# Token-ordered rows with indirect loads, column sums of the first weights off TensorE, and a sixth key/value slot in a fused attention and Fourier feed-forward kernel

## The chip, the cores and the metric

The kernel runs on one core of one Trainium2 chip. The metric is the device time of one launch in microseconds (us). A core has TensorE (PE in the profile; PEld is its weight load), VectorE (DVE), ScalarE (ACT), GpSimd (POOL) and SyncE (SP), which issues most DMAs. Each engine works through its own queue in order.

## The reference

Two stages follow one another. The first is linear attention with a norm over each head, the second mixes each sequence by a two-dimensional Fourier transform, normalises each row, and adds a feed-forward of width 2048. All is float32; 8 sequences of 576 tokens, 8 heads of 64, model width 512. The weights come as float64.

```python
kv = np.einsum('bhsd,bhse->bhde', k, v)
out = np.einsum('bhsd,bhde->bhse', q, kv)
rms = np.sqrt(np.mean(out * out, axis=-1, keepdims=True) + 1e-06)
out = out / rms * g_norm                      # -> x, (8, 576, 512)
...
X = np.fft.fft(np.fft.fft(x, axis=1), axis=2)
u = x + np.real(X)
mu, var = u.mean(-1), u.var(-1)
un = (u - mu) / np.sqrt(var + 1e-06)
ch = np.maximum(un @ w_ch1, 0.0) @ w_ch2
return u + ch
```

## The kernel before, in words

**Two phases.** Phase one takes the sequences one after the other: key/value products (`plan_kv`), query turns (`plan_q`), attention output (`plan_out`), head norm (`plan_y`, `plan_fold`), the transform along the sequence (`plan_seq`) and along the channels (`plan_chn`). The finished rows u go to a DRAM scratch `u_scr`, and their transposes (`plan_turn`) as a high and a low float32r part into blocks of 512 tokens, `unTh` and `unTl`; nine blocks in all. A feed-forward product is three matmuls, high by high, high by low, low by high (`passes`, `ffn1` L341, `ffn2` L360). While phase one runs, `plan_early` already multiplies each finished block by the first three of sixteen feed-forward slices (`NA = 3`) and saves the partial sums. Phase two is the loop at L1168: over segments (block, first slice, last slice); each step makes one slice of the hidden layer (`first`, 12 matmuls of 512 columns) and multiplies the slice of the step before by the second weights (`second`, 12 more).

**The halves of a sequence.** Phase one keeps a sequence as two halves, s = 1..288 in rising order and s = 575..289 in falling order, so that the transform can use the symmetry of sine and cosine (`side` 0 and 1). Before the change that order stays: `u_scr`, the token blocks, the partial sums and the mean row `p0c` all have the second half of each sequence reversed, and the true place is restored at the very end. `ascending(t)` (L224) tells whether a tile of 128 rows lies wholly in first halves; 12 of the 36 tiles do. Those are stored by a direct DMA from SP (L1157); the other 24 by an indirect DMA from POOL (L1159) which scatters rows by `rowidx`.

**The weights.** Each weight slice arrives as float64 words and is turned to float32 by a copy on ACT and six operations on DVE (`w_clear` L281, `w_steps` L283, a total). From a slice of the first weights the mean over the 512 inputs is taken off, since the row mean then need not be subtracted from u: `w_mean` (L302) multiplies each of the four 128-column pieces by a matrix of 1/512 and sums them in PSUM (four float32 matmuls, which the trace shows as eight records), `w_center` subtracts on DVE. Then ACT copies the high part and DVE (phase one, L850) or POOL (phase two, L1071) makes the low part. In phase one this is `plan_w` (L822), for slices 0 to 2 at the start and 3 to 6 once the queries, keys and values are through; in phase two `load_w`, `sum_w` and `split_w` (L1048 to L1071) for slices 7 to 15, one weight slice a step over the first 18 steps.

**What sets the order.** Phase one is written down as operations with a cost, a rank and the buffers they need, and a planner (`Plan`, L54) simulates the engines at build time: at every moment each engine takes the ready operation of lowest rank for which ring slots are free, and the program is emitted in that order. Ring sizes stand in `RINGS` (L37): five slots `kv` of 256 KB for keys and values, two slots `wk` for work tiles of weights, eight PSUM banks `p8`. Phase two is a plain loop. The framework then schedules the emitted program by a simulation of its own and adds the waits. Phase two's rows are read back from `u_scr` (`load_u` L1099), in a ring `uu` of eight tiles, that is, two blocks; their variance is taken on DVE (L1107), and POOL adds in the scaled early partial sums (L1119). After the last slice of a block DVE adds the product (L1153) and the tile is stored.

Of the kernel before, what the change touches and what calls it, by code (L numbers as in the profile page):

```python
# [9 lines left out]
F32 = mybir.dt.float32  # L10
# [21 lines left out]

PAD_LEFT = 32
# [4 lines left out]
    "p8": 8, "part": 2, "unT": 2, "h": 2 * NA, "qt": 2, "fq": 4, "kvt": 2, "kv": 5, "kr": 2,  # L38
# [15 lines left out]
class Plan:  # L54
# [16 lines left out]
    def op(self, eng, cost, rank, emit, after=(), bufs=(), lag=0, port=False):  # L71
        o = Op()
        o.port = port or eng == "POOL"
        o.eng, o.cost, o.rank, o.emit, o.lag = eng, cost, rank, emit, lag
# [14 lines left out]
    def run(self):  # L89
# [20 lines left out]
        while left:  # L110
# [14 lines left out]
            while again:  # L125
                again = False
                for eng, q in ready.items():
# [40 lines left out]
                    for u in users[o.n]:  # L168
                        need[u.n] -= 1
                        if not need[u.n]:  # L170
# [4 lines left out]
                            heapq.heappush(events, (max(at, t), n, "ready", u))  # L175
# [6 lines left out]
def kernel(  # L182
# [119 lines left out]
    def w_mean(ps, af):  # L302
        for c in range(KC):
            nc.tensor.matmul(  # L304
                ps[:, :P], mean_t, af[:, c * P : (c + 1) * P], start=(c == 0), stop=(c == KC - 1)
            )
# [472 lines left out]
    def plan_turn(b, side, t, x, done):  # L779

        n = TR + 1 if side == t == 0 else TR - 1 if side and t == 2 else TR
        r0 = b * S + (HALF + 1 if side else 1) + t
        cols = [(0, min(n, TR), r0, 3)] + [(TR, n, b * S, 1)] * (n > TR)
        pieces = []
        for lo, hi, at, step in cols:
            while lo < hi:
                j = at // BT
                end = min(hi, lo + -(-((j + 1) * BT - at) // step))
# [16 lines left out]
        for j, lo, hi, at, step in pieces:  # L805
            to = slice(at, at + step * (hi - lo - 1) + 1, step)
# [15 lines left out]
    def plan_w(which, f, pool, r, after=(), r_load=None):  # L822
# [11 lines left out]
        d = op("ACT", 670, r, lambda: w_clear(raw.t, ps.t), [a], [raw, ps, pf])  # L834
# [13 lines left out]
        def lo(src):  # L848
            h, l = w_t[which, f]
            nc.vector.tensor_tensor(l, src.t, h.bitcast(F32), ALU.subtract)  # L850

        src = ps
        if which == 1:
            src, mean = ring("wk", one, [P, DM], "wa"), bank_buf("ps_w")
            e = op("DVE", 700, r, lambda: total(src), [d], [src, ps, pf])
            e = op("PE", 870, r, lambda: w_mean(mean.t, src.t), [e], [src, mean])
# [4 lines left out]
        w_done[which, f] = op("DVE", 700, r, lambda: lo(src), [g], [src], port=(which == 1))  # L861
# [117 lines left out]
    def p0_out():  # L979
# [5 lines left out]
        nc.vector.tensor_copy(p0u.t[:B, : HALF - 1], p0t.t[:B, 1:HALF])  # L985
# [66 lines left out]
    def sum_w(which, f):  # L1052
# [7 lines left out]
        sums[which, f] = af  # L1060

    def split_w(which, f):
        af = sums.pop((which, f))
        if which == 1:
            ps = bank("ps_w")
            w_mean(ps, af)
# [71 lines left out]
    def second(seg, hpair, f):  # L1138
        j, f0, f1 = seg
        for i in tiles_of[j]:  # L1140
# [15 lines left out]
            if ascending(t):  # L1156
                nc.sync.dma_start(out[t * P : (t + 1) * P, :], ut)  # L1157
            else:
# [115 lines left out]
```

## Time and profile before

| | |
|---|---|
| median of 3 runs | 1050.78 us (1050.68 to 1051.03) |
| the profiled execution | 1044.39 us, of which the span from first to last instruction is 1042.5 us |
| mean granted TensorE clock | 0.993 |
| TensorE matmul busy | 1003.8 us, 5962 records |
| DVE, ACT, POOL busy | 472.9, 325.7, 310.9 us |
| DMA moved | 140.72 MB |

The page splits the span into 40 slices of 26 us each; a digit gives the busy share in tenths. Phase one fills about the first 15 slices, the loop the rest. Busy times of DVE instructions overlap a little (0.69 us long, started every 0.60 us), so a sum of them is more than the time they take. Some matmul records are missing from the trace, so a PE share just under 1 in a long dense window is not idle time. In the chain of waits the share of an engine says how much of the span it was the last to be ready.

### The profile page before, as it was taken

To read this page: it belongs to the slowest core of one execution; us is meant where nothing else is said; L and a number is where in the kernel's file an instruction comes from. 1 tells how busy PE (TensorE), PEld (TensorE's weight loads), DVE (VectorE), ACT (ScalarE), POOL (GpSimd) and SP (SyncE) were. 2 spreads that over 40 slices of the span, in tenths; PEclk is the share of its full clock that TensorE was granted. 3 is DMA by queue.
4 is the path that set the end of the run, shared out by engine and by line. 5 is a ranking of instruction groups with operands and counts; after the bars stand their busy time and mean duration, and the time that the engine had idled before them with its cause. 6 is when DMAs were issued, how large, how long until landed. Compare 5 with 4: busy or idle time off the path is not lost.

```text
span 1042.5 us, 15216 instructions
## 1 busy us (share of the span) xinstructions
PE 1003.8 (96%) x5962; PEld 847.3 (81%) x5962; DVE 472.9 (45%) x830; ACT 325.7 (31%) x655; POOL 310.9 (30%) x316
## 2 busy tenths in 40 slices
PE   4799999999999899999999999999999999999996
PEld 4687888889878788888888888888888888888884
DVE  4878466667498758887132313131221311311111
ACT  3566556555543334334212022121121121111110
POOL 0466966774662001113813111130020010110000
PEclk9999999999999999999999999999999999999998
DMA  9969688663345845634552414240230400400101
GB/s 251 256 165 283 164 255 243 199 163 130 129 144 201 303 156 194 234 123 141 174 177 75 162 45 158 90 134 20 102 100 1 162 21 1 162 1 1 41 0 41
DMA packets 109195, 140.72 MB, mean 135 GB/s; under 512 B 51790, under 2 KB 76418, under 8 KB 104516
## 3 DMA queue, kind: packets, MB, share of 16 engines
q1 hardware_dynamic: 105588, 132.28, 41.1%
q0 software_dynamic: 1920, 6.29, 1.5%
q10 hardware_dynamic: 1616, 1.18, 0.4%
q8 instruction: 47, 0.77, 0.3%
q14 instruction: 24, 0.20, 0.1%
HBM read 88.33 MB, written 51.40 MB: 134 GB/s over the span
## 4 chain that ended last, share of the span: by engine, by line
PE 88%; DVE 5%; DMA 3%; POOL 2%; issue 1%; ACT 1%; SPq 0%; POOLq 0%; ACTq 0%; DVEq 0%
PE ps_h L345 37%; PE acc L363 37%; PE ps_f L684 3%; PE ps_f L718 3%; PE ps_o L545 3%; PE ps_k L472 2%; PE ps_q L520 1%; PE ps_w L304 1%; PE ps_t L801 1%; DMA vm<-in_v_dram 1%; DMA qt<-in_q_dram 1%; DVE x L642 1%; DVE wp L298 1%; POOL xe L660 0%; DVE ps_a L288 0%
## 5 line engine op out<-in xcount | busy, mean ns | idle before, releaser
L345 PE MATMUL ps_h<-unTh,w 128*128 128x512 f32 x1152 | 357.1, 391 | 0.0
L363 PE MATMUL acc<-w,hh 128*128 128x512 f32 x1152 | 354.7, 393 | 0.0
L358 DVE SCALAR_TENSOR_TENSOR hl<-ps_h,hh 128x512 fp32r<-128x512 f32 x144 | 99.1, 688 | 370.0 <-ACT hh L355 369.8
L363 PEld LDWEIGHTS acc<-w,hh 128*128 128x128 f32 x1152 | 215.9, 189 | 44.7
L345 PEld LDWEIGHTS ps_h<-unTh,w 128*128 128x128 f32 x1152 | 215.0, 188 | 44.0
L355 ACT ACTIVATE hh<-ps_h 128x512 fp32r<-128x512 f32 x144 | 85.8, 596 | 454.3 <-PE ps_h L345 449.0
L345 PE MATMUL ps_h<-unTl,w 128*128 128x512 f32 x576 | 224.5, 390 | 0.0
L363 PE MATMUL acc<-w,hl 128*128 128x512 f32 x576 | 221.3, 391 | 0.0
L1159 POOL DMA_INDIRECT out_dram<-uu,rowidx x24 | 23.4, 975 | 390.4 <-DVE uu L1153 345.1
L363 PEld LDWEIGHTS acc<-w,hl 128*128 128x128 f32 x576 | 108.6, 189 | 22.8
L345 PEld LDWEIGHTS ps_h<-unTl,w 128*128 128x128 f32 x576 | 108.0, 188 | 22.7
L580 POOL TENSOR_TENSOR x<-x,gb 96x512 f32<-96x512 f32 (+1 forms) x48 | 61.1, 1297 | 43.4 <-ACT x L560 43.4
L1119 POOL TENSOR_TENSOR uu<-uu,up 128x512 f32<-128x512 f32 x36 | 45.6, 1292 | 58.2 <-ACT up L1116 58.2
L1071 POOL TENSOR_TENSOR w<-wap,w 128x512 fp32r<-128x512 f32 x18 | 23.0, 1296 | 132.2 <-ACT w L1070 122.7
L545 PE MATMUL ps_o<-kvt,fq 64*96 64x64 f32 (+1 forms) x768 | 45.8, 269 | 1.4 <-ACT fq L524 0.9
L1107 DVE BATCH_NORM_STATS2 bst<-uu 128x6 f32<-128x512 f32 x36 | 24.7, 691 | 48.4 <-DMA uu<-u_scr 48.4
L545 PEld LDWEIGHTS ps_o<-kvt,fq 64*96 64x96 f32 (+1 forms) x768 | 41.9, 180 | 5.3 <-issue 1.4
L1153 DVE SCALAR_TENSOR_TENSOR uu<-acc,rs_yb,uu 128x512 f32<-128x512 f32 x36 | 25.2, 744 | 42.5 <-PE acc L363 42.5
L660 POOL TENSOR_TENSOR xe<-ab 96x256 f32<-96x256 f32 (+1 forms) x48 | 38.8, 834 | 18.4 <-DVE ab L653 12.1
L569 DVE TENSOR_REDUCE ss<-ps_o 96x8 f32<-96x512 f32 (+1 forms) x48 | 31.7, 682 | 22.1 <-ACT ps_o L565 20.5
L472 PE MATMUL ps_k<-vm,km 128*64 128x64 f32 x512 | 27.6, 252 | 13.0 <-DMA vm<-in_v_dram 13.0
L684 PE MATMUL ps_f<-cs,xh 96*128 96x290 f32 (+1 forms) x192 | 39.2, 300 | 0.0
(98 smaller groups left out, 1012.9 us busy)
## 6 DMA issues: line engine op xcount, KB each, us to landing
raw<-in_moe_w_ch_dram SPq DMA_DIRECT2D x32, 512.0 KB
qt<-in_q_dram SPq DMA_DIRECT2D x16, 576.0 KB
unT_scr<-unTh SPq DMA_DIRECT2D x9, 1024.0 KB
unT_scr<-unTl SPq DMA_DIRECT2D x9, 1024.0 KB
part_scr<-part SPq DMA_DIRECT2D x36, 256.0 KB
uu<-u_scr SPq DMA_DIRECT2D x36, 256.0 KB
unTh<-unT_scr SPq DMA_DIRECT2D x9, 1024.0 KB
unTl<-unT_scr SPq DMA_DIRECT2D x9, 1024.0 KB
```

What stands on the lines that cost most here:

```text
L345: nc.tensor.matmul(ps, w[c][:, kc * P : (kc + 1) * P], unT[a][:, kc, :], start=(idx == 0), stop=(idx == 3 * KC - 1),)
L355: nc.scalar.activation(hh, ps, AF.Relu)
L358: nc.vector.scalar_tensor_tensor(hl, ps, 0.0, hh.bitcast(F32), ALU.max, ALU.subtract)
L363: nc.tensor.matmul(acc, hpair[a][:, i * P : (i + 1) * P], w[c], start=(first and n == 0), stop=(last and n == 2),)
L472: nc.tensor.matmul(ps.t[s * D : (s + 1) * D, pr * D : (pr + 1) * D], km[:, s, j, :] if j < 4 else kr[:, h, :], vm[:, s, j, :] if j < 4 els ...
L545: nc.tensor.matmul(pss[s].t[:n, at : at + D], fqs[side].t[half, m, :n], kvt.t[half, m], start=True, stop=True,)
L569: nc.vector.tensor_reduce(ss.t[0][:n, :, t, s::2], pss[s].t[:n].rearrange("p (u m e) -> p u m e", u=2, e=D), AX.X, ALU.add,)
L580: nc.gpsimd.tensor_tensor(v_, v_, gb[:n].unsqueeze(1).to_broadcast([n, H, D]), ALU.mult)
L660: nc.gpsimd.tensor_tensor(o[:, s], a[:, 0], a[:, 1], ALU.subtract if s else ALU.add)
L684: nc.tensor.matmul(ps.t[:, :NS], xs[t].t[a][:n, part, ch * P : (ch + 1) * P], cs[:n, part, c, t, :], start=(idx == 0), stop=(idx == 8),)
L718: nc.tensor.matmul(ps.t[:n, :ND], pt.t[a][:, part, ch, offs[t] : offs[t] + n], cd[:, part, c, ch, :], start=(idx == 0), stop=(idx == 5),)
L1119: nc.gpsimd.tensor_tensor(us[j][i], us[j][i], part, ALU.add)
```

## The change

- The transposes of the second half are written in falling columns (`plan_turn`), and the mean row is reversed once on DVE, so token blocks, partial sums and outputs have the order of the tokens. `u_scr` keeps the old order. All 36 tiles are stored by direct DMAs from SP; the 24 tiles that aren't ascending are instead gathered from `u_scr` by indirect loads on POOL in `load_u`.
- `w_mean` becomes one matmul on a tile of 128 columns. The sum of the four pieces that feeds it is made before: by one DVE reduction for slices 0 to 2 and 7 to 15, by three POOL additions for slices 3 to 6. For slices 3 to 6 POOL also makes the low part of the first weights in place of DVE.
- In the planner, `w_mean` counts as ready 2000 ns later than its input (`SLACK`), and a slice of the first weights claims both of its work tiles at once, at the copy on ACT.
- The ring `kv` has six slots in place of five.

```diff
+SLACK = 2000
...
-    ... "kvt": 2, "kv": 5, "kr": 2,
+    ... "kvt": 2, "kv": 6, "kr": 2,
...
-    def op(self, eng, cost, rank, emit, after=(), bufs=(), lag=0, port=False):
+    def op(self, eng, cost, rank, emit, after=(), bufs=(), lag=0, port=False, wait=0):
...
-                            heapq.heappush(events, (max(at, t), n, "ready", u))
+                            heapq.heappush(events, (max(at, t) + u.wait, n, "ready", u))
...
-    def w_mean(ps, af):
-        for c in range(KC):
-            nc.tensor.matmul(
-                ps[:, :P], mean_t, af[:, c * P : (c + 1) * P], start=(c == 0), stop=(c == KC - 1)
-            )
+    def w_sum(af, to):
+        nc.vector.tensor_reduce(to, af.rearrange("p (c n) -> p n c", c=KC), AX.X, ALU.add)
+
+    def w_sum_pool(af, to):
+        nc.gpsimd.tensor_tensor(to, af[:, :P], af[:, P : 2 * P], ALU.add)
+        for c in range(2, KC):
+            nc.gpsimd.tensor_tensor(to, to, af[:, c * P : (c + 1) * P], ALU.add)
+
+    def w_mean(ps, total):
+        nc.tensor.matmul(ps[:, :P], mean_t, total, start=True, stop=True)
...
-        r0 = b * S + (HALF + 1 if side else 1) + t
-        cols = [(0, min(n, TR), r0, 3)] + [(TR, n, b * S, 1)] * (n > TR)
+        if side:
+            cols = [(0, n, b * S + S - 1 - t, -3)]
+        else:
+            cols = [(0, min(n, TR), b * S + 1 + t, 3)] + [(TR, n, b * S, 1)] * (n > TR)
...
-        d = op("ACT", 670, r, lambda: w_clear(raw.t, ps.t), [a], [raw, ps, pf])
+        src = ring("wk", one, [P, DM], "wa") if which == 1 else ps
+        d = op("ACT", 670, r, lambda: w_clear(raw.t, ps.t), [a], [raw, ps, pf, src])
+        late_ = f >= NA
...
-            nc.vector.tensor_tensor(l, src.t, h.bitcast(F32), ALU.subtract)
+            eng = nc.gpsimd if late_ and which == 1 else nc.vector
+            eng.tensor_tensor(l, src.t, h.bitcast(F32), ALU.subtract)
...
-            e = op("PE", 870, r, lambda: w_mean(mean.t, src.t), [e], [src, mean])
+            if late_:
+                e = op("POOL", 2000, r, lambda: w_sum_pool(src.t, pf.t[:, :P]), [e], [src, pf])
+            else:
+                e = op("DVE", 600, r, lambda: w_sum(src.t, pf.t[:, :P]), [e], [src, pf])
+            e = op("PE", 220, r, lambda: w_mean(mean.t, pf.t[:, :P]), [e], [pf, mean], wait=SLACK)
...
-        nc.vector.tensor_copy(p0u.t[:B, : HALF - 1], p0t.t[:B, 1:HALF])
+        nc.vector.tensor_copy(p0u.t[:B, : HALF - 1], p0t.t[:B, HALF - 1 : 0 : -1])
...
-        sums[which, f] = af
+        if which == 1:
+            w_sum(af, pf[:, :P])
+        sums[which, f] = af, pf[:, :P]
...
-            nc.sync.dma_start(ut, u_scr[n * P : (n + 1) * P])
+            if ascending(n):
+                nc.sync.dma_start(ut, u_scr[n * P : (n + 1) * P])
+            else:
+                nc.gpsimd.indirect_dma_start(
+                    out=ut,
+                    out_offset=None,
+                    in_=u_scr[:NTOK],
+                    in_offset=bass.IndirectOffsetOnAxis(ap=rowidx[:, n : n + 1], axis=0),
+                )
...
-            if ascending(t):
-                nc.sync.dma_start(out[t * P : (t + 1) * P, :], ut)
-            else:
-                nc.gpsimd.indirect_dma_start(
-                    out=out,
-                    out_offset=bass.IndirectOffsetOnAxis(ap=rowidx[:, t : t + 1], axis=0),
-                    in_=ut,
-                    in_offset=None,
-                )
+            nc.sync.dma_start(out[t * P : (t + 1) * P, :], ut)
```

More of the change, by code (lines that the diff above doesn't have):

```diff
@@ L37 @@
 RINGS = {
-    "p8": 8, "part": 2, "unT": 2, "h": 2 * NA, "qt": 2, "fq": 4, "kvt": 2, "kv": 5, "kr": 2,
+    "p8": 8, "part": 2, "unT": 2, "h": 2 * NA, "qt": 2, "fq": 4, "kvt": 2, "kv": 6, "kr": 2,
     "x": 8, "raw": 2, "e2": 4, "wk": 2, "xhl": 3, "pt": 1, "two": 2,
@@ L69, in __init__ @@
         self.now = 0
-    def op(self, eng, cost, rank, emit, after=(), bufs=(), lag=0, port=False):
+    def op(self, eng, cost, rank, emit, after=(), bufs=(), lag=0, port=False, wait=0):
         o = Op()
         o.port = port or eng == "POOL"
+        o.wait = wait
         o.eng, o.cost, o.rank, o.emit, o.lag = eng, cost, rank, emit, lag
@@ L787, in plan_turn @@
                 j = at // BT
-                end = min(hi, lo + -(-((j + 1) * BT - at) // step))
+                last = (j + 1) * BT - 1 if step > 0 else j * BT
+                end = min(hi, lo + (last - at) // step + 1)
                 pieces.append((j, lo, end, at - j * BT, step))
@@ L805, in plan_turn @@
         for j, lo, hi, at, step in pieces:
-            to = slice(at, at + step * (hi - lo - 1) + 1, step)
+            stop = at + step * (hi - lo - 1) + (1 if step > 0 else -1)
+            to = slice(at, None if stop < 0 else stop, step)
             def high(j=j, lo=lo, hi=hi, to=to):
@@ L849, in lo @@
             h, l = w_t[which, f]
-            nc.vector.tensor_tensor(l, src.t, h.bitcast(F32), ALU.subtract)
-        src = ps
+            eng = nc.gpsimd if late_ and which == 1 else nc.vector
+            eng.tensor_tensor(l, src.t, h.bitcast(F32), ALU.subtract)
         if which == 1:
-            src, mean = ring("wk", one, [P, DM], "wa"), bank_buf("ps_w")
+            mean = bank_buf("ps_w")
             e = op("DVE", 700, r, lambda: total(src), [d], [src, ps, pf])
-            e = op("PE", 870, r, lambda: w_mean(mean.t, src.t), [e], [src, mean])
+            if late_:
[3 more added lines that the diff above has]
+            e = op("PE", 220, r, lambda: w_mean(mean.t, pf.t[:, :P]), [e], [pf, mean], wait=SLACK)
             e = op("DVE", 690, r, lambda: w_center(src.t, mean.t), [e], [src, mean])
@@ L860, in plan_w @@
         g = op("ACT", 640, r, lambda: hi(src), [e], [src])
-        w_done[which, f] = op("DVE", 700, r, lambda: lo(src), [g], [src], port=(which == 1))
+        pool_lo = late_ and which == 1
+        w_done[which, f] = op(
+            "POOL" if pool_lo else "DVE", 1340 if pool_lo else 700, r, lambda: lo(src), [g], [src],
+            port=(which == 1),
+        )
     last_first = []
```

5 lines of the change are left out of this document (3 added, 2 removed).

## The prediction, made before the changed kernel was run

> **What bounds the kernel now.** I read the page's busy times and slices first, then the windows by stage, then the waits of TensorE, then the timeline where it waits.
>
> ```profile
> PE 1003.8 (96%) x5962; PEld 847.3 (81%) x5962; DVE 472.9 (45%) x830; ACT 325.7 (31%) x655; POOL 310.9 (30%) x316
> PE   4799999999999899999999999999999999999996
> DVE  4878466667498758887132313131221311311111
> ```
>
> ```profile
> 0.00:58.00 58.00, 37.23 (x388) 33.29 (x390) 33.85 (x55) 25.03 (x50) 19.07 (x31) 1.00 1.00 241
> 58.00:387.00 329.00, 321.36 (x2700) 279.00 (x2697) 230.77 (x421) 171.38 (x393) 179.92 (x192) 0.99 0.63 195
> 387.00:491.00 104.00, 104.00 (x496) 87.17 (x495) 85.90 (x127) 41.92 (x70) 21.70 (x17) 1.00 0.53 178
> 491.00:1031.60 540.60, 540.60 (x2386) 447.61 (x2385) 119.61 (x225) 87.33 (x144) 88.32 (x75) 1.00 0.24 80
> 1031.60:1042.50 10.90, 0.62 (x3) 0.19 (x1) 2.73 (x4) 0.00 (x0) 1.92 (x2) 0.65 0.24 96
> ```
>
> The second fence gives window, length, busy time of PE, PEld, DVE, ACT and POOL with counts, then granted clock, DMA share and GB/s. There are five stages. Up to 58 us TensorE is fed too slowly (37 of 58 us busy) and the DMA engines are full (share 1.00). From 58 to 387 us it is busy for all but 7.6 us. In the two loop windows it is never idle. In the last 10.9 us it has nothing left, and the clock runs on after the last matmul. So time comes out in three ways: matmuls taken off TensorE after 58 us, gaps of TensorE closed, and a shorter end.
>
> **Part 1: the mean of the first weights, in the loop.** Nine slices (7 to 15) lie here.
>
> ```profile
> 407.06 1.06 PE L304 MATMUL ps_w<-wap,mean_t 128*128 128x128 f32 x8
> 407.87 0.70 PE L345 MATMUL ps_h<-unTh,w 128*128 128x512 f32 x2
> 408.11:419.94 11.83, 11.83 (x58) 9.91 (x57) 10.35 (x16) 6.04 (x10) 2.55 (x2) 1.00 0.93 322
> 499.11:509.99 10.88, 10.88 (x49) 9.01 (x49) 1.38 (x2) 4.47 (x6) 10.88 (x10) 1.00 0.61 182
> ```
>
> Two steps with a mean in them take 11.83 us, two without 10.88, so a mean costs 0.95 us. Its eight records start within 407.87 - 407.06 = 0.81 us, 0.101 each; a float32 matmul is two of them, 0.203 us. Three of four go: 0.61 us each, and the remaining 0.34 (one matmul and the change of operands) stays. 9 x 0.61 = 5.5 us. If the whole 0.95 shrinks in proportion, 9 x 0.71 = 6.4.
>
> What is added is a DVE reduction over four pieces 512 bytes apart. No row shows that stride; the nearest is the reduction of adjacent elements below, 680 ns. DVE was busy 10.35 us in the 11.83 (overlaps counted twice). With 0.68 more it is 11.03, against a new TensorE period of 11.83 - 0.61 = 11.22. It fits, narrowly. If the strided read takes twice as long, 1.36, DVE needs 11.71 and becomes the bound: 0.49 x 9 = 4.4 us of the 5.5 are lost. I take 5.5, because 512 elements per partition are read in both; ends 1.1 and 6.4.
>
> **Part 2: the same in phase one.** Slices 2 to 6 lie after 58 us, where other matmuls always wait: 5 x 0.61 = 3.0 us (ends 0, if some other wait eats it, and 3.5). One of the five has a gap in front:
>
> ```profile
> 348.88 2.05 PE L304 MATMUL ps_w<-wa,mean_t 128*128 128x128 f32 x8 [3.42 <-DVE wa L842]
> 345.40:348.90 3.50, 0.08 (x2) 0.05 (x1) 3.40 (x6) 0.60 (x1) 0.00 (x0) 0.99 1.04 438
> 348.90:352.60 3.70, 3.70 (x14) 3.33 (x15) 2.69 (x5) 0.69 (x2) 0.00 (x0) 0.55 0.97 345
> ```
>
> The mean stood at the head of TensorE's queue 3.42 us before DVE had the total, and behind it stood matmuls that could have run. The clock granted afterwards is 0.55 for 3.70 us: another 3.70 x 0.45 = 1.7 us. Together 5.1. The planner's SLACK puts the mean 2.0 us later in the order, so a DVE that is as late as before leaves a gap of 1.4; other matmuls that now come first may close that too. Ends: 5.1 gained, or 5.1 lost, since a new order may leave such a gap elsewhere. I take 3.4, between 2.0 and 5.1. [...]
>
> POOL's share for slices 3 to 6 hides behind its own idleness: it is idle from 345.40 to 352.60 (0.00 twice). Prices:
>
> ```profile
> L569 DVE TENSOR_REDUCE ss<-ps_o 96x8 f32<-96x512 f32 x32 | 21.0, 680 | 14.5 <-ACT ps_o L565 13.0 <-PE ps_q L520 1.5
> L660 POOL TENSOR_TENSOR xe<-ab 96x256 f32<-96x256 f32 x32 | 26.4, 845 | 2.0 <-DVE ab L653 1.3 <-ACT xh L666 0.7
> L609 POOL TENSOR_TENSOR rs_s<-rs_y,m x8: 286/288/291, 42.9 to 285.2; 97x48 f32<-97x48 f32 x8
> L1071 POOL TENSOR_TENSOR w<-wap,w 128x512 fp32r<-128x512 f32 x18 | 23.0, 1296 | 132.2 <-ACT w L1070 122.7 <-issue 9.5
> 287.32 0.68 DVE L288 TENSOR_SCALAR ps_a<-ps_a 128x512 f32<-128x512 f32 x1
> 359.04 0.69 DVE L850 TENSOR_TENSOR w<-wa,w 128x512 fp32r<-128x512 f32 x1 [0.70 <-ACT w L846]
> 401.77 1.36 PE ps_h L345 x6
> ```
>
> A POOL addition of 128 columns lies between 0.29 (48 columns) and 0.85 (256); I take 0.45. Each slice becomes later by 2.0 (SLACK), 3 x 0.45 = 1.4, 1.30 - 0.69 = 0.6 for the low part on POOL, and about 6 x 0.68 = 4.1 because with both work tiles claimed at once the second weights no longer overlap: 8.1 us, 32 for the four. The last low part of slice 6 was done at 359.04 + 0.69 = 359.7; the loop first uses it at 401.77. Cover 42 us, so this costs nothing. Reversed columns in ACT and DVE writes keep their element counts: nothing taken.
>
> **Part 3: the start.**
>
> ```profile
> 21.71 2.07 PE L304 MATMUL ps_w<-wa,mean_t 128*128 128x128 f32 x8
> 23.58 0.85 PE L520 MATMUL ps_q<-ident,qt 96*128 96x96 f32 x4
> 38.17 0.48 PE L472 MATMUL ps_k<-vr,kr 64*64 64x64 f32 x4 [3.04 <-DMA vr<-in_v_dram]
> 42.95 1.12 PE L472 MATMUL ps_k<-vm,km 128*64 128x64 f32 x16 [2.84 <-DMA vm<-in_v_dram]
> SPq L451 <- PE ps_k L472: 2.8, 2, 2.3
> km<-in_k_dram SPq DMA_DIRECT2D x32, 256.0 KB
> ```
>
> Slices 0 and 1 run on a slow TensorE: 1.87 us for eight records (21.71 to 23.58), so six fewer save 1.4 each, 2.8 together, less two reductions of 0.68 on a DVE that is the next bound here: 1.4. But TensorE waits for loads at 38 and 42 us, so part of that is only waited out. The sixth slot can remove at most the 2.8 us that SP waited for a slot. It adds no bandwidth: the engines are full, and 256 KB moved ahead of something more urgent costs 256 KB / 241 GB/s = 1.1 us. I take 1.0 for the whole start; ends -2.5 (1.1 and the reductions lost) and +5.6.
>
> **Part 4: order of rows, and the end.**
>
> ```profile
> 1031.65 2.73 DVE L1153 SCALAR_TENSOR_TENSOR uu<-acc,rs_yb,uu 128x512 f32<-128x512 f32 x4 [3.51 <-PE acc L363]
> 1032.68 0.96 POOL L1159 DMA_INDIRECT out_dram<-uu,rowidx  x1 [64.94 <-DVE uu L1153]
> 1036.12 0.96 POOL L1159 DMA_INDIRECT out_dram<-uu,rowidx  x1 [2.48 <-DMA out_dram<-uu,rowidx]
> 1039.35 0.38 SPq L1157 DMA_DIRECT2D out_dram<-uu  x1
> ```
>
> The last results are ready at 1031.65 + 2.73 = 1034.38. But the second scatter waits for the first to land, and the direct stores wait for the second, since a scatter may write any row of `out`. The last direct store is issued at 1039.35, and the span ends 3.15 us later. With four direct stores to separate rows nothing waits: last issue near 1034.5, end 1037.65. Gain 4.85 us; 4.3 if the four transfers queue.
>
> Inside the loop the scatters go and 24 gathers come on the same POOL queue; each is followed in program order by the variance on DVE, with `hl` for the next step behind it.
>
> ```profile
> L1159 POOL DMA_INDIRECT out_dram<-uu,rowidx x24 | 23.4, 975 | 390.4 <-DVE uu L1153 345.1 <-DVE bmv L1108 15.4 <-DMA out_dram<-uu,rowidx 15.3
> DVE bst L1107 <- DMA uu<-u_scr: 48.4, 27, 3.2
> 405.22 0.69 DVE L358 SCALAR_TENSOR_TENSOR hl<-ps_h,hh 128x512 fp32r<-128x512 f32 x1 [2.15 <-ACT hh L355]
> 410.72 0.62 PE L363 MATMUL acc<-w,hh 128*128 128x512 f32 x2
> ```
>
> DVE waits for these rows today too, 27 times, at most 3.2 us. `hl`, ready at 405.91, is first used after the two matmuls at 410.72, so it has about 5 us in hand. Gathers don't write `out` or `u_scr`, so they need not follow one another. Cost nothing; the cover is those 5 us.
>
> **Sum.** 5.5 + 3.0 + 3.4 + 1.0 + 4.85 = 17.75 us. The profiled execution took 1044.39 us, a span of 1042.5 and 1.9 around it; it becomes 1026.6. The median of the runs, 1050.78, lies 6.4 above the profiled one; I take the same saving from it: 1033.0.
>
> **The rivals.** *Only loop and end pay.* Before 387 us a saving is real only while TensorE has other work; if loads at the start and DVE's lateness set the pace of phase one, parts 2 and 3 are waited out. For it: the gaps at 38, 42 and 345 us are all on others. Against: only 7.6 idle us in 329. It leaves 5.5 + 4.85 = 10.35: 1040.4.
>
> *The weights of slices 3 to 6 come late.* If each mean also waits for a chain of twelve matmuls ahead of it (10.88 / 4 = 2.7), the 32 us become 43, and DVE work that piles up adds to it. With some 6 us beyond the cover, and the 3.4 of the gap not gained, 1033.0 + 9.4 = 1042.4. What speaks for more is this row:
>
> ```profile
> 412.22 1.33 DVE L298 SCALAR_TENSOR_TENSOR wap<-raw,wap 128x512 f32<-128x512 uint32 x1
> ```
>
> A DVE operation on two SBUF tiles takes 1.33 beside POOL's low part. [...]
>
> *Slower: gathers in series.* If each gather waits for the one before, as the scatters do (1036.12 - 1032.68 = 3.44 apart), and the scheduler puts three variances ahead of one `hl`, DVE holds it 10.3 us against 5 in hand: 5.3 us of idle TensorE for each of seven blocks (27 waits today are about seven times four tiles), 37 us, so 1070. It decides from a hold of about 7.6 us, 2.5 a block, that is, from the third gather. Against: gathers only read, and today's longest wait is 3.2.
>
> **How the numbers follow.** Forecast 0.66, only loop and end 0.18, late weights 0.06, gathers in series 0.06, anything else 0.04. Range: the tops of the terms make 6.4 + 3.5 + 5.1 + 5.6 + 4.85 = 25.4, 1025.4, all at once unlikely, so from 1026; upward to the late weights, 1043. A measurement can tell about 0.2%, 2.1 us: faster 0.90 (the first three cases but for a little of each, and half of the rest), same 0.03, slower 0.07.
>
> **What would show it.** In the changed profile: two records of `ps_w` per first weight, a period near 11.2 us in the loop; no wait of a store for another and about 3.2 us from the last DVE result to the end; 58 to 387 us shortened by some 6 us without a gap at a mean; the start about as long as now. I am wrong if the loop's period stays near 11.8 (DVE), if a gap before a `ps_f` or `ps_h` stands behind weights of slices 3 to 6, or if TensorE shows idle time between blocks with DVE waiting for `uu`.

## The result, and the profile after

The changed kernel takes 1026.39 us (median of six runs, 1025.23 to 1028.47) beside 1050.9 us for the kernel before in the same comparison (six runs, 1045.84 to 1056.77). The ratio is 0.9765 with an interval of 0.9733 to 0.9798: 24.5 us faster, where 17.75 were forecast. The profiled execution went from 1044.39 to 1026.22 us, its span from 1042.5 to 1024.4, its mean clock from 0.993 to 0.996. So the two profiles are 18.1 us apart, and the two medians 24.5. Both need an answer.

The page of the changed kernel, busy times and two rows of the slices:

```profile
PE 993.9 (97%) x5866; PEld 839.4 (82%) x5866; DVE 472.0 (46%) x838; ACT 322.4 (31%) x655; POOL 320.6 (31%) x332
PE   4698999999999999999999999999999999999998
PEclk9998999999999999999999999999999999999999
```

TensorE is still the bound, with 9.9 us less to do. The windows by stage, cut where the stages of this kernel change (window, length, busy PE, PEld, DVE, ACT, POOL with counts, clock, DMA share, GB/s):

```profile
0.00:58.00 58.00, 36.70 (x382) 31.79 (x383) 32.57 (x52) 24.70 (x50) 20.41 (x32) 1.00 1.08 238
58.00:380.70 322.70, 318.52 (x2661) 278.87 (x2662) 224.03 (x396) 170.71 (x391) 191.87 (x211) 0.99 0.65 196
380.70:491.00 110.30, 110.30 (x497) 91.59 (x496) 97.07 (x168) 45.28 (x80) 35.83 (x29) 1.00 0.57 197
491.00:1018.75 527.75, 527.75 (x2331) 436.97 (x2330) 115.58 (x220) 81.76 (x135) 72.48 (x62) 1.00 0.23 78
1018.75:1024.40 5.65, 0.61 (x3) 0.18 (x1) 2.73 (x4) 0.00 (x0) 0.00 (x0) 0.79 0.48 186
```

To split the 18.1 us, two landmarks serve that both traces have. The first is the start of the loop, the first chain of 24 matmuls into `ps_h` that no work of phase one interrupts. It stands in the chain of waits, first of before, then of after:

```profile
387.25 5.44 PE ps_h L345 x24
```

```profile
380.72 5.44 PE ps_h L354 x24
```

The second is the start of DVE's last four operations on `uu`: 1031.65 in before (the row stands in the prediction) and, in the timeline of after,

```profile
1018.78 2.73 DVE L1186 SCALAR_TENSOR_TENSOR uu<-acc,rs_yb,uu 128x512 f32<-128x512 f32 x4 [3.51 <-PE acc L372]
1019.56 2.31 SPq L1189 DMA_DIRECT2D out_dram<-uu  x4
```

- **Phase one:** 387.25 to 380.72, 6.5 us less.
- **Loop:** 1031.65 - 387.25 = 644.40 becomes 1018.78 - 380.72 = 638.06, 6.3 us less.
- **End:** 1042.5 - 1031.65 = 10.85 becomes 1024.4 - 1018.78 = 5.62, 5.2 us less.

**The loop.** Two windows of the loop in after, two steps with one mean in them and two with none:

```profile
402.95:414.07 11.12, 11.12 (x52) 9.24 (x51) 10.83 (x17) 4.65 (x9) 2.59 (x2) 1.00 0.84 294
497.12:508.00 10.88, 10.88 (x50) 9.01 (x49) 1.38 (x2) 2.01 (x3) 8.29 (x8) 1.00 0.67 191
```

The mean now costs 11.12 - 10.88 = 0.24 us in place of 0.95. TensorE stays busy in the whole window, and DVE in 10.83 of 11.12. The groups show what was added:

```profile
L1133 POOL DMA_INDIRECT uu<-u_scr,rowidx x24 | 23.4, 974 | 286.2 <-DVE uu L1186 175.6 <-DVE bmv L1141 61.1 <-DMA out_dram<-uu 41.0
L307 DVE TENSOR_REDUCE wap<-wap 128x128 f32<-128x512 f32 x9 | 9.8, 1089 | 0.2
L312 POOL TENSOR_TENSOR wp<-wp,wa 128x128 f32<-128x128 f32 x8 | 3.7, 461 | 0.6
```

**Phase one.** The gap of 3.42 us in front of a mean is gone: near its place, the mean at 352.88 comes without a pause. What TensorE still waits for up to the loop are almost only loads, and one of these waits has grown (timeline of TensorE in after, lines left out between):

```profile
45.39 0.91 PE L481 MATMUL ps_k<-vm,km 128*64 128x64 f32 x12 [8.27 <-DMA vm<-in_v_dram]
...
91.99 1.12 PE L481 MATMUL ps_k<-vm,km 128*64 128x64 f32 x16 [3.03 <-DMA vm<-in_v_dram]
...
352.88 0.39 PE L315 MATMUL ps_w<-wp,mean_t 128*128 128x128 f32 x2
```

Idle time of TensorE, from the windows: 58.00 - 36.70 = 21.3 us at the start (before 20.8) and 322.70 - 318.52 = 4.2 from there to the loop (before 7.6).

Idle time is not the whole price of a wait, since the clock can fall around it. In after the clock is 0.50 from 90.22 to 97.04 us, around the wait of 3.03 us at 91.99; in before it is 1.00 there. And at the start TensorE is slow for longer, although the clock column reads 1.00 in both. The same sixteen matmuls, first in before, then in after:

```profile
55.17 0.71 PE L472 MATMUL ps_k<-vm,km 128*64 128x64 f32 x16
```

```profile
56.42 1.12 PE L481 MATMUL ps_k<-vm,km 128*64 128x64 f32 x16
```

In before they take 1.12 us up to 47.17; in after they take 0.69 when they are next seen, at 69.71. In the second profile of before (kernel 1), whose clock column has 0.50 from 40 to 50 us, they take 1.12 as well, at 46.82. So two numbers describe phase one: the idle time of TensorE, and its busy time for the same matmul records, which grows where the clock is slow. Up to the start of the loop before has 358.8 us busy and 28.4 idle, after 355.2 and 25.5.

### The profile page after: what moved, and what is told of

Read it like the earlier page. It is cut to its first block, busy times and chain, and to the rows that moved or that the text cites. A ratio compares the mean times of both kernels' runs of the same rounds, so it can differ in the third digit from the quotient of the medians.

```text
span 1024.4 us, 15026 instructions
## 1 busy us (share of the span) xinstructions
PE 993.9 (97%) x5866; PEld 839.4 (82%) x5866; DVE 472.0 (46%) x838; ACT 322.4 (31%) x655; POOL 320.6 (31%) x332
## 4 chain that ended last, share of the span: by engine, by line
PE 93%; DMA 2%; DVE 2%; SPq 1%; issue 1%; ACT 0%; POOL 0%; DVEq 0%; ACTq 0%; POOLq 0%
PE ps_h L354 38%; PE acc L372 38%; PE ps_o L554 4%; PE ps_f L727 3%; PE ps_f L693 3%; PE ps_k L481 3%; PE ps_q L529 2%; PE ps_t L813 2%; DMA vm<-in_v_dram 2%; DVE x L651 1%; DMA qt<-in_q_dram 1%; SPq L510 1%; PE ps_w L315 0%; SPq L460 0%; DVE unTl L825 0%
## 5 line engine op out<-in xcount | busy, mean ns | idle before, releaser
L372 PE MATMUL acc<-w,hh 128*128 128x512 f32 x1152 | 345.0, 391 | 0.2 <-DVE unTl L825 0.2
L372 PE MATMUL acc<-w,hl 128*128 128x512 f32 x576 | 213.1, 390 | 0.0
L1133 POOL DMA_INDIRECT uu<-u_scr,rowidx x24 | 23.4, 974 | 286.2 <-DVE uu L1186 175.6
L693 PE MATMUL ps_f<-cs,xh 96*128 96x290 f32 (+1 forms) x192 | 41.8, 312 | 0.4 <-DVE x L651 0.4
L481 PEld LDWEIGHTS ps_k<-vm,km 128*64 128x64 f32 x512 | 22.9, 166 | 22.4 <-DMA km<-in_k_dram 16.2
```

The source lines that it names most:

```text
L372: nc.tensor.matmul(acc, hpair[a][:, i * P : (i + 1) * P], w[c], start=(first and n == 0), stop=(last and n == 2),)
L481: nc.tensor.matmul(ps.t[s * D : (s + 1) * D, pr * D : (pr + 1) * D], km[:, s, j, :] if j < 4 else kr[:, h, :], vm[:, s, j, :] if j < 4 els ...
L693: nc.tensor.matmul(ps.t[:, :NS], xs[t].t[a][:n, part, ch * P : (ch + 1) * P], cs[:n, part, c, t, :], start=(idx == 0), stop=(idx == 8),)
```

## The experiments

Twelve kernels ran, in three groups; each group had its own runs of the kernel before beside it. The two last columns come from the profiled execution of each: the first record of a mean in the loop (394.34 in before, 387.82 in after), and the time from there to the end of the span. That cuts phase one from everything behind it.

| kernel | median, us | before beside it | ratio, interval | first mean of the loop | from there to the end |
|---|---|---|---|---|---|
| before (first profile) | 1050.90 | | | 394.34 | 648.16 |
| changed | 1026.39 | 1050.90 | 0.9765, 0.9733 to 0.9798 | 387.82 | 636.58 |
| 1 before, again | 1051.40 | 1049.45 | 0.9991, 0.9950 to 1.0031 | 401.91 | 648.09 |
| 2 direct stores on before | 1046.91 | 1050.00 | 0.9983, 0.9959 to 1.0007 | 398.01 | 643.19 |
| 3 order of rows on before | 1050.18 | 1049.45 | 0.9998, 0.9966 to 1.0030 | 406.14 | 642.96 |
| 4 changed, direct loads | 1025.08 | 1050.28 | 0.9773, 0.9726 to 0.9819 | 386.93 | 635.17 |
| 5 loop mean on before | 1042.60 | 1049.45 | 0.9935, 0.9895 to 0.9975 | 398.24 | 641.76 |
| 6 changed, sum twice | 1027.25 | 1050.28 | 0.9790, 0.9744 to 0.9836 | 386.76 | 637.74 |
| 7 weights of phase one on before | 1042.23 | 1050.00 | 0.9926, 0.9908 to 0.9944 | 392.04 | 648.16 |
| 8 changed, no slack | 1034.41 | 1050.00 | 0.9866, 0.9839 to 0.9893 | 394.76 | 636.64 |
| 9 changed, slack 4000 | 1026.52 | 1050.28 | 0.9777, 0.9729 to 0.9825 | 387.48 | 636.62 |
| 10 changed, POOL's share on DVE | 1033.41 | 1050.28 | 0.9835, 0.9782 to 0.9887 | 397.49 | 635.71 |
| 11 sixth slot on before | 1054.01 | 1050.00 | 1.0046, 1.0030 to 1.0063 | 403.87 | 648.13 |
| 12 changed, five slots | 1029.66 | 1049.45 | 0.9795, 0.9735 to 0.9854 | 391.74 | 636.66 |

In kernels 4 and 10 the order puts the first mean of the loop at another place among the matmuls of its step, up to 1.4 us away; for these the start of the loop is used below. The interval of a ratio is as wide as it is mostly because the kernel before scatters.

### 1. The kernel before, once more

No edit. The question is where the 6.4 us between its profiled execution and its median lie.

> The kernel before, unchanged, taken as a kernel of its own: it gives a second profile of it. The profiled execution of before took 1044.4 us, its other runs 1045.8 to 1056.8, while the changed kernel's six runs lie between 1025.2 and 1028.5. Theory: the 6.4 us between profile and median of before are a gap of TensorE in phase one whose length depends on when loads land, so this profile shows another size of it, with the time from the first matmul of the loop (387.25 us in the first profile) to the end unchanged within 1 us. Rival: the difference is spread over the whole span (clock or matmul pitch); then the loop itself is longer.

Its ten runs go from 1044.27 to 1058.66, and this profile has a span of 1050.0 where the first had 1042.5. From the first mean to the end the two agree to 0.1 us (648.09 and 648.16; spans are known to 0.1). All 7.5 us lie in phase one. The timeline of TensorE in this run:

```profile
37.57 0.48 PE L472 MATMUL ps_k<-vr,kr 64*64 64x64 f32 x4 [5.97 <-DMA vr<-in_v_dram]
...
110.82 0.29 PE L472 MATMUL ps_k<-vr,kr 64*64 64x64 f32 x2 [2.15 <-DMA vr<-in_v_dram]
```

The first wait was 3.04 in the first profile. After the second the clock falls. The window from 100 to 120 us, of the first profile and of this one:

```profile
100.00:120.00 20.00, 19.02 (x193) 16.65 (x193) 11.81 (x18) 12.60 (x29) 19.27 (x21) 1.00 0.67 177
```

```profile
100.00:120.00 20.00, 17.86 (x123) 15.27 (x121) 11.55 (x16) 8.30 (x20) 15.70 (x18) 0.83 0.62 162
```

Clock 0.83 instead of 1.00 costs 20 x 0.17 = 3.4 us, and TensorE idles 1.2 us more. The 3.4 is an estimate, like every loss of clock here: the length of a window times what its clock is short of 1.00. The pace of the matmuls agrees: in the first profile six of 512 columns take 310.37 - 307.72 = 2.65 us in a stretch of clock 0.50, and six behind it 312.84 - 311.47 = 1.37. So the same program is late by a load, and pays again in clock. The mean's gap of 3.42 is in both profiles. Loop and end are the same in both profiles; phase one is not, by loads and the clock behind them. So the median of the kernel before seems to contain such misses, its first profile hardly any; only the two profiles show where the time lies.

### 2. Direct stores alone

```diff
-            if ascending(t):
-                nc.sync.dma_start(out[t * P : (t + 1) * P, :], ut)
-            else:
-                nc.gpsimd.indirect_dma_start(...)
+            nc.sync.dma_start(out[t * P : (t + 1) * P, :], ut)
```

> The kernel before with all 36 tiles stored by direct DMAs, so the second halves of the output stay reversed; no gathers, and phase one's program untouched. Theory: the end alone gets shorter by 5.2 us, and the row-order part lost this again in phase one because reversed columns change the planner's order there (first mean of the loop at 406 us). So here 5.2 us faster than before at the same phase one: span 1037 to 1045, median ratio 0.995. Rival: the end's gain is not real in the median; then the time equals before's within 0.2%.

From the first mean to the end it takes 643.19 us, 4.97 less than before; the timeline's last rows are

```profile
1035.32 2.73 DVE L1153 SCALAR_TENSOR_TENSOR uu<-acc,rs_yb,uu 128x512 f32<-128x512 f32 x4 [3.50 <-PE acc L363]
1036.10 2.31 SPq L1156 DMA_DIRECT2D out_dram<-uu  x4
```

The four stores are issued one per result, and the span of 1041.2 us ends 1041.2 - 1035.32 = 5.9 us after DVE's first of the four, where before needed 10.85. That the stores waited for scatters is shown as the cause. The runs' ratio is 0.9983, with 1 inside the interval: phase one's scatter covers a gain of 5 us, and only the split shows it.

### 3. The order of rows alone

```diff
-        r0 = b * S + (HALF + 1 if side else 1) + t
-        cols = [(0, min(n, TR), r0, 3)] + [(TR, n, b * S, 1)] * (n > TR)
+        if side:
+            cols = [(0, n, b * S + S - 1 - t, -3)]
+        else:
+            cols = [(0, min(n, TR), b * S + 1 + t, 3)] + [(TR, n, b * S, 1)] * (n > TR)
...
+            (gathers in load_u, direct stores at the end, as in the change)
```

> The kernel before with the row order alone changed: falling columns, indirect loads in place of indirect stores, all stores direct. Theory: only the end gets shorter, by 5.2 us as the two traces show (10.9 us after the last matmul become 5.7); phase one and the loop stay within 1 us, so a span of 1037.3 us. Rival: taking the scatters away also frees the loop or phase one (more than 8 us), or the gathers cost there (less than 3 us).

Behind the first mean it gains 5.2 us, as forecast, with 24 gathers in the loop. But its first mean is at 406.14, and the runs show no gain. The reversed columns change which blocks a piece of a sequence falls into, and the planner writes another order. In it the mean comes still earlier than its input:

```profile
359.88 2.04 PE L304 MATMUL ps_w<-wa,mean_t 128*128 128x128 f32 x8 [4.92 <-DVE wa L846]
```

That is 1.5 us more than the 3.42 of before. Two waits for keys and values at 93.28 and 96.94, 2.54 and 2.71 us, are longer too, and a gap of 1.21 us near 305 in before is one of 2.46 at 315.25. The forecast had put the reversed columns at nothing, since they keep their element counts. Their own cost is nothing as far as these runs show (the 80 writes of `unTl` on DVE have a median of 511 ns, 508 in before); their effect on the order was some 8 us beside the mean of the four profiles that have the phase one of before (394.3, 401.9, 398.0 and 398.2, mean 398.1). It is waits: up to the start of the loop TensorE idles 40.5 us, where those four have 28.4 to 33.1, and is busy for 358.5, where they have 358.0 to 362.6.

### 4. The changed kernel without gathers

```diff
-            if ascending(n):
-                nc.sync.dma_start(ut, u_scr[n * P : (n + 1) * P])
-            else:
-                nc.gpsimd.indirect_dma_start(...)
+            nc.sync.dma_start(ut, u_scr[n * P : (n + 1) * P])
```

> The changed kernel with all rows read from the scratch by direct DMAs, so the second halves get u of other rows; no gather anywhere. Theory: the gathers are hidden, as the changed profile's loop shows no idle TensorE: span within 1 us of 1024.4, first mean of the loop within 1 us of 387.8. Rival: the gathers cost a wait for each block that the schedule hides in phase one; then 2 us or more are gained.

The median is 1.3 us below the changed kernel's. The loop starts at 378.47, and DVE's last chain stands at

```profile
1016.53 2.73 DVE L1178 SCALAR_TENSOR_TENSOR uu<-acc,rs_yb,uu 128x512 f32<-128x512 f32 x4 [3.50 <-PE acc L372]
```

From the start of the loop that is 638.06 us, to the hundredth what the kernel with gathers needs. So the gathers cost nothing in the loop, and what differs lies ahead of it: 354.1 us busy and 24.4 idle in place of 355.2 and 25.5, with 3.41 us of slow clock near 91 us in place of 6.82. The waits of DVE's variance for its rows, from 491 us to the end, with gathers and then without (engine and line, what it waited for: total, times, longest):

```profile
DVE bst L1140 <- DMA uu<-u_scr,rowidx: 17.6, 16, 1.9
...
DVE bst L1140 <- DMA uu<-u_scr: 8.7, 4, 3.0
```

```profile
DVE bst L1132 <- DMA uu<-u_scr: 32.2, 21, 3.7
```

In these two runs a gather holds DVE no longer than a direct load does: 1.9 us at most, against 3.7.

### 5. The loop's mean alone

```diff
+        if which == 1:
+            w_sum(af, pf[:, :P])
-        sums[which, f] = af
+        sums[which, f] = af, pf[:, :P]
...
-            w_mean(ps, af)
+            w_mean1(ps, tot)
```

Phase one keeps its four matmuls a mean; `w_mean1` is the changed `w_mean` under another name.

> The kernel before with the sum of the columns on DVE and one matmul in the loop alone (slices 7 to 15); phase one as before. Theory: the loop's period falls from 11.83 to 11.12 us, 9 x 0.71 = 6.4 us, span 1036.1 us, and DVE is not the bound. Rival: the scheduler's simulation moves other work too, and the loop gains less than 5 us.

648.16 becomes 641.76, 6.40 us or 0.71 for each of nine slices: a mean loses six of its eight records and with them three quarters of the whole 0.95, not only of the 0.81 in which the records start. The medians are 6.9 us apart. With the end's 5.2 this gives 648.16 - 6.40 - 5.2 = 636.6, and the changed kernel has 636.58: the two parts add up.

### 6. The sum made twice

```diff
         if which == 1:
             w_sum(af, pf[:, :P])
+            w_sum(af, pf[:, P : 2 * P])
```

> The changed kernel with the DVE column sum of the loop done twice (the second result isn't used). In the changed profile the strided sum takes 1.09 us, not the 0.68 forecast, and DVE is busy 10.1 to 11.1 of a period of 11.12 us. Theory: DVE is then close to being the bound, so a second sum makes the period about 11.6 to 12.2 us and the kernel 4 to 9 us slower. Rival: overlapped starts leave DVE more room than its busy time says; then the period stays at 11.12 and the time within 1.5 us.

The theory that DVE is all but full, so that a second sum must lengthen the period by most of its length, fell: 1027.25 us, not to be told from the changed kernel by the medians, and 1.2 us longer behind the first mean. The windows of the loop's first weights, of the changed kernel and then of this one:

```profile
387.82:425.19 37.37, 37.37 (x170) 31.10 (x169) 36.04 (x69) 15.11 (x29) 7.78 (x6) 1.00 0.60 216
425.19:480.00 54.81, 54.81 (x248) 45.48 (x247) 48.53 (x77) 22.99 (x42) 15.01 (x12) 1.00 0.53 179
```

```profile
386.76:425.23 38.47, 37.99 (x170) 30.87 (x169) 37.65 (x71) 15.78 (x30) 7.78 (x6) 1.00 0.58 204
425.23:480.00 54.77, 54.77 (x247) 45.42 (x246) 54.60 (x85) 23.99 (x42) 15.86 (x13) 1.00 0.55 186
```

The same matmuls take 1.1 us more in the first window, once, where a mean waits for its sum; behind it TensorE is never idle although DVE is busy for 54.60 of 54.77 us. In the changed kernel DVE had 54.81 - 48.53 = 6.3 us free in these five periods, about 1.25 each, and a second sum takes 1.0. The 10.83 of 11.12 in the window from 402.95 us, and the 10.35 of 11.83 on which the prediction built, came from one early period, in which DVE was behind; the five that follow show four times that room. Two sums all but fill DVE; that a third would pass the limit is an estimate from these figures, no run has it.

### 7. The weights of phase one alone

The whole of `plan_w` as in the change, on the kernel before (sums on DVE and POOL, one matmul a mean, `SLACK`, both work tiles claimed at the copy); loop, order of rows and slots stay.

```diff
-            e = op("PE", 870, r, lambda: w_mean(mean.t, src.t), [e], [src, mean])
+            if late_:
+                e = op("POOL", 2000, r, lambda: w_sum_pool(src.t, pf.t[:, :P]), [e], [src, pf])
+            else:
+                e = op("DVE", 600, r, lambda: w_sum(src.t, pf.t[:, :P]), [e], [src, pf])
+            e = op("PE", 220, r, lambda: w_mean1(mean.t, pf.t[:, :P]), [e], [pf, mean], wait=SLACK)
```

> The kernel before with the weights of phase one alone changed (column sums on DVE and POOL, one matmul a mean, SLACK, both work tiles claimed at once, low parts on POOL); loop, row order and five slots as before. Theory: phase one loses 21 matmuls (7 x 0.71 = 5 us) and the gap near 345 us (5 us): first mean of the loop at 384 to 392 us against 394.3 and 401.9 in two profiles of before, loop and end unchanged (648.1 us after it), span 1032 to 1040. Rival: without the other parts the planner's new order opens other gaps and the phase gains less than 4 us against the mean of the two profiles (398).

The medians are 7.8 us apart; the first mean of the loop stands at 392.04, 6 us below the four profiles' mean of 398.1, where the theory had 10, and the rest is that of before. The mean that had the gap runs without one (the first mean, at 17.18 us, has one of 1.36, in a stretch that waits for loads):

```profile
354.39 0.39 PE L319 MATMUL ps_w<-wp,mean_t 128*128 128x128 f32 x2
```

### 8. The changed kernel with no slack

```diff
-SLACK = 2000
+SLACK = 0
```

> The changed kernel with SLACK = 0: a mean of phase one is again ready for the planner as soon as its input is. Theory: the gap of TensorE in front of a mean near 345 us, with the slow clock behind it, comes back in part, since POOL's planned 2000 ns for additions that the changed profile shows at 3 x 0.46 us already give 0.6 us: 1 to 5 us more than the changed kernel, phase one (start to the first mean of the loop, 387.8 us) 389 to 393 us. Rival: SLACK did nothing, the gap was closed by the new place of the sum; then it stays within 1 us with no gap in front of a mean.

The cost is 7 to 8 us (1034.41 beside 1026.39, spans 1031.4 and 1024.4), more than was expected. The gap is back:

```profile
352.65 0.49 PE L315 MATMUL ps_w<-wp,mean_t 128*128 128x128 f32 x2 [2.67 <-POOL wp L312]
```

It brings the slow clock with it. The windows behind it begin at the end of the gap:

```profile
352.65:354.00 1.35, 1.35 (x7) 1.12 (x8) 0.69 (x1) 0.10 (x1) 0.00 (x0) 0.94 0.99 419
354.00:356.00 2.00, 2.00 (x6) 1.61 (x5) 0.00 (x0) 0.53 (x1) 1.28 (x1) 0.50 0.96 350
356.00:358.00 2.00, 2.00 (x7) 1.55 (x6) 0.00 (x0) 0.49 (x1) 0.00 (x0) 0.69 1.03 346
358.00:362.00 4.00, 4.00 (x19) 3.32 (x18) 3.11 (x5) 2.27 (x5) 0.00 (x0) 1.00 0.30 115
```

1.35 x 0.06 + 2 x 0.50 + 2 x 0.31 = 1.7 us, so the gap costs 2.67 + 1.7 = 4.4 in all. The loop starts 6.9 us later (387.66 against 380.72): TensorE idles 2.9 us more, nearly all of it this gap, and is busy 4.1 us longer for the same 3041 records. Of these 4.1, 1.7 lie behind the gap; the rest fits a slow start that lasts longer (the sixteen `ps_k` matmuls still take 1.12 us at 56.76 and are next seen, with 0.69, at 72.40, where the changed kernel has 69.71), but no run isolates it. The wait at 45 us is 1.1 longer, 9.34 in place of 8.27, but other waits of the start are shorter: up to 58 us the idle time differs by 0.45.

### 9. Twice the slack

```diff
-SLACK = 2000
+SLACK = 4000
```

> The changed kernel with SLACK = 4000. Theory: 2000 already closes the gap in front of the means, so more only lets the planner's order differ: within 3 us either way, no gap in front of a mean. Rival: the more slack the better; then 2 us or more faster than the changed kernel.

1026.52 beside 1026.39: no difference. There is no gap before a mean left to close. The two orders are not the same, though: up to the loop this one idles 21.8 us in place of 25.5 and is busy for 358.6 in place of 355.2.

### 10. POOL's share back on DVE

```diff
-        late_ = f >= NA
+        late_ = False
```

> The changed kernel with the sums and low parts of slices 3 to 6 on DVE in place of POOL, planned at 600 and 700 ns. Theory: what counts is the mean's later place in the order; DVE has room near 345 us, so the time stays within 3 us of the changed kernel, with a small gap (under 2 us) in front of a mean possible because the planned 2000 ns on POOL is gone. Rival: POOL's share is what frees DVE there; then 4 us or more slower with a gap of 2.5 us or more in front of a mean.

The theory (within 3 us) fell, its rival held but for a hair in the gap (2.47 us, where it had 2.5 or more): 7 us slower by the medians, the loop starts at 389.49 in place of 380.72. With the sum planned for 600 ns on DVE rather than 2000 on POOL, the mean is placed earlier, and DVE is later than planned:

```profile
352.49 0.46 PE L315 MATMUL ps_w<-wp,mean_t 128*128 128x128 f32 x2 [2.47 <-DVE wp L307]
```

```profile
350.00:352.50 2.50, 0.03 (x2) 0.04 (x1) 2.27 (x3) 0.00 (x0) 0.00 (x0) 1.00 0.97 406
352.50:354.00 1.50, 1.50 (x6) 1.28 (x7) 1.01 (x2) 0.29 (x1) 0.00 (x0) 0.76 1.10 453
354.00:356.00 2.00, 2.00 (x6) 1.56 (x5) 1.97 (x4) 0.34 (x1) 0.00 (x0) 0.50 0.98 412
356.00:358.00 2.00, 2.00 (x8) 1.60 (x8) 1.90 (x4) 0.00 (x0) 0.00 (x0) 0.82 1.00 416
```

DVE works 2.27 of these 2.50 us and POOL none: it is DVE's queue that the mean waits for, as in before. Price again 2.47 + 1.7 = 4.2. From the start of the loop to DVE's last chain it takes 638.06 us, as the changed kernel does, so all of the loss is in phase one. Gaps of 0.95 and 0.64 at 297 and 314 us and 0.9 more at 92 come on top, and around that last wait the clock is slow for 10.24 us where the changed kernel has 6.82. In sum TensorE idles 4.6 us more up to the loop and is busy 4.2 longer for the same 3041 records. Whether the work on POOL or its longer planned cost closes the gap, this run doesn't tell apart.

### 11. The sixth slot alone

```diff
-    ... "kvt": 2, "kv": 5, "kr": 2,
+    ... "kvt": 2, "kv": 6, "kr": 2,
```

> The kernel before with six key/value slots and nothing else. Theory: the slot shortens waits of TensorE for loads between 80 and 120 us, where the kernel before goes slow after them; phase one gains 2 to 5 us against 398 (mean of two profiles of before), loop and end unchanged. Rival: it only moves the waits to 45 us, and the time stays within 2 us of before.

Neither theory held: alone, the slot makes the kernel before 4 us slower, and the interval leaves 1 out. Its timeline has a wait for loads nearly as long as that of the changed kernel, and the gap in front of the mean:

```profile
44.91 1.12 PE L472 MATMUL ps_k<-vm,km 128*64 128x64 f32 x16 [7.45 <-DMA vm<-in_v_dram]
```

```profile
361.34 1.71 PE L304 MATMUL ps_w<-wa,mean_t 128*128 128x128 f32 x8 [2.87 <-DVE wa L842]
```

Yet it does not wait longer: TensorE idles 29.9 us up to the loop, where the four profiles have 30.7 on average. It is busy for 366.9 us, where they have 360.3 with the same 3083 records. The largest slow stretch follows a wait of 1.82 us for POOL, and its window shows the clock:

```profile
134.27 0.55 PE L801 MATMUL ps_t<-ident,x 96*128 96x96 f32 x4 [1.82 <-POOL x L748]
```

```profile
136.44:150.09 13.65, 13.65 (x90) 12.40 (x90) 9.64 (x19) 6.64 (x17) 6.26 (x11) 0.50 0.94 286
```

At half the clock that is 13.65 x 0.50 = 6.8 us. So the slot alone loses its time to the clock.

### 12. The changed kernel with five slots

```diff
-    ... "kvt": 2, "kv": 6, "kr": 2,
+    ... "kvt": 2, "kv": 5, "kr": 2,
```

> The changed kernel with five key/value slots again. Theory: the sixth slot adds no bandwidth and only reorders loads; in the changed profile TensorE waits 8.3 us for one load at 45 us, so five slots give the same time or up to 4 us less (0 to -4 us against the changed kernel's 1024.4 us span). Rival: the sixth slot is what feeds phase one; then five slots cost 3 us or more.

Here the slot is worth 3.3 us by the medians and 3.9 by the start of the loop (384.64 against 380.72), the size that the rival gave. The windows up to the loop, of the changed kernel and of this one:

```profile
0.00:380.72 380.72, 355.24 (x3041) 310.68 (x3042) 256.61 (x447) 195.40 (x440) 212.28 (x242) 0.99 0.72 202
```

```profile
0.00:384.64 384.64, 358.00 (x3041) 312.35 (x3042) 248.34 (x446) 195.77 (x440) 212.01 (x242) 0.98 0.71 200
```

The same matmuls are busy 2.8 us longer, and TensorE idles 1.2 more. So most of it is clock, not feeding: around the waits near 90 us the clock is slow for 17.06 us (87.73 to 104.79) in place of 6.82. The same edit costs 4 us in one program and gains 3 to 4 in the other.

## Why the prediction was right, and where it was not

**Part 1, the loop.** Right in kind and sign. The 5.5 us were a count of removed matmuls; the whole 0.95 shrank, 0.71 each, and 6.3 to 6.4 came, the upper end. Two prices in it were off without consequence: the sum takes 1.09 us, not 0.68, and DVE's margin, called narrow, holds a second sum for all slices but the first.

**Part 2, the means of phase one.** The 3.4 us for the gap were too careful: the gap closed whole, 3.42 us and the slow clock of 1.7, and the gap of 1.4 us that was foreseen did not come. What keeps it closed are the slack (kernel 8) and the move to POOL (kernel 10); without either it is back at 2.5 to 2.7. A shorter gap was not cheaper in clock: those of 2.47 us (kernel 10) and 2.67 (kernel 8) paid the same 1.7 us, estimated from the windows, as the one of 3.42. The trace of before already had a second slow stretch, behind two short gaps, which the working did not count and which is gone in after:

```profile
305.25 0.55 PE L801 MATMUL ps_t<-ident,x 96*128 96x96 f32 x4 [1.21 <-DVE hl L358]
306.67 1.09 PE L801 MATMUL ps_t<-ident,x 96*128 96x96 f32 x8 [0.87 <-DVE wa L842]
```

```profile
307.84:311.25 3.41, 3.41 (x9) 2.65 (x10) 3.41 (x9) 3.05 (x10) 0.46 (x1) 0.50 0.21 76
```

That is 1.21 + 0.87 + 1.7 = 3.8 us that the forecast did not have. For the five means' 3.0 us there is no run of its own; matmul busy time up to the loop fell from 358.8 to 355.2, which holds them and the clock's part together. The cover of 42 us for the late weights was enough: in the profile of after neither `ps_h` nor `acc` waits for a weight.

**Part 3, the start.** The gain of 1.0 us did not come: TensorE idles 21.3 us up to 58 us (20.8 before) and is slow for longer, the wait at 91.99 us came with a slow clock (0.50 for 6.82 us), and the first `ps_h` stands at 95.34 in place of 87.70. The step that failed is the price of the sixth slot: its ends, 2.8 us won and 1.1 lost, were taken from SP's wait for a slot and from the bandwidth of one transfer, while it acts through the order that the planner writes and the clock that this order gets, from 4 us lost (kernel 11) to 3 or 4 won (kernel 12) with the rest of the program.

**Part 4, the end.** Right: 5.2 us for 4.85, by kernels 2 and 3 as well. The last result to the end of the span took 1024.4 - (1018.78 + 2.73) = 2.9 us, where 0.1 and 3.15 had been put.

**The sum** of 17.75 us met the two profiles' 18.1, in part by luck: phase one gave 6.5 us where 3.0 + 3.4 + 1.0 = 7.4 were put, but in it the mean's gap came back whole, 3.8 us came that were not in the sum, and the start and the wait at 91.99 lost where 1.0 was to be won. **The median** did not follow it: the same saving was taken from 1050.78, on the assumption that the 6.4 us between profile and median are the same for both kernels. Kernel 1 shows a second profile that is late by load misses of phase one and the clock behind them; the changed kernel's six runs scatter by 3.2 us only, so it seems to have fewer. So 24.5 us came, and the forecast of 1033.0 was 6.6 too high, near the low end of its range. Why the misses are rarer is open. The four kernels with the old weights plan and five slots scatter by 7.6 to 14.4 us in ten runs each, the eight others by 1.3 to 6.1 in four (of the ten, the first four alone scatter by 4.4 to 10.5, so part of the difference is the number of runs); the slot alone and the weights alone each are in the second set, so it is not one part's doing.

**Why the parts don't add up in phase one.** By the medians, the parts alone give: order of rows +0.7, loop -6.9, weights -7.8, slot +4.0, together -10. The whole gives -24.5. Loop and end are additive in all profiles; the other 14 us lie in phase one, in whose order the slot alone costs some 4 us and the reversed columns alone some 6 by the medians (0.7 and the 5.2 of the end) or 8 by the profile, and in the whole they don't. Alone, both keep the gap in front of the mean (2.87 and 4.92 us beside 3.42), at most 1.5 us more. The rest is of two kinds: the reversed columns idle 9.8 us longer than the four profiles' mean of 30.7 and are busy 1.8 less; the slot idles 0.8 less and is busy 6.6 longer, by the clock. Why these orders get these waits and this clock was not isolated.

**The rivals.** *Only loop and end pay* fell, since phase one gave 6.5 us even beside the faster of the two profiles of before. *Late weights* did not occur. *Gathers in series* fell to kernel 4. That rival's argument took over the scatters' distance of 3.44 us, where the second waits 2.48 us for the first to land. Gathers don't write the tensor that the next one reads, and in the trace of after two of them start 577.15 - 575.89 = 1.26 us apart, though the quickest of the 24 takes 3.3 us to land.

## What to carry to other kernels

On TensorE, which is never idle in the loop, the matmuls removed were paid in full with their change of operands (0.71 us a mean in kernel 5, where the count of matmuls alone gave 0.61). Stores whose rows are only known at run time held up later stores to the same tensor (10.85 us from DVE's last chain to the end in before, 5.9 with direct stores in kernel 2); a gather of the same rows held nothing up here (638.06 us for the loop with gathers and without, kernel 4). A mean that stood ahead of its input in TensorE's queue cost the gap and the slow clock behind it (3.42 us and an estimated 1.7 in before), so plan such a matmul late. Where a planner writes the order, try parts in combination, look at the stages apart, compare idle time and the busy time of the same matmuls separately, and take a profile of the old kernel more than once before believing its distance to the median.

## What the runs showed of the hardware

- **A strided sum.** The reduction of 512 elements to 128 over pieces 512 bytes apart takes 1.09 us on DVE (L307 in after); the reduction of as many adjacent elements took 0.68 (L569 in before). That is (1089 - 680) / 512 = 0.8 ns more for each element read. But the two reductions also differ in what they write, 128 elements and 8, and in where they read, `wap` in SBUF and `ps_o` in PSUM, and no run parts these.
- **The clock after short gaps.** Idle gaps of 2.47 and 2.67 us (kernels 10 and 8) were followed, within 1.5 us after work had resumed, by a clock of 0.50 for 2 us and of 0.69 to 0.94 on either side, 1.7 us lost each time by the estimate above. Behind the gaps of 2.87 us in kernel 11 and 4.92 in kernel 3 the clock is 0.50 as well, from 363 to 365 and from 359.9 to 364 us. Between 70 us and the loop before has two slow stretches of 3.41 us, from 307.84 and from 348.80, and after has one of 6.82, from 90.22, all at a clock of 0.50. Of the gaps near 1 us some have it and some not: those of 1.21 and 0.87 us at 305.25 and 306.67 in before were followed by 3.41 us of slow clock, while around those of 1.11 us at 90.22 and 0.98 at 106.31 in the same trace it is 1.00. The price varies too: the wait of 3.03 us in after has 6.82 us of slow clock around it, the gap of 3.42 in before 3.41.
- **One period is not the loop.** DVE was busy for 96% of the window from 387.82 to 425.19 us and for 89% of the next five periods. A margin read from the first would have forbidden what the second allows.
